# Thirty small loads that nobody reads, in two sets on SyncE's queue, in a decode attention kernel

## The chip, the cores and the metric

The kernel runs on one core of a Trainium2 chip. The metric is the device time of one execution in microseconds (us); the time shown is the median of three runs. The profile and the trace belong to one further execution, taken by the hardware profiler, and all times inside it count from its first instruction.

## The reference

One decode step of grouped-query attention, gated by a small dense network. With B = 2 sequences, one query position each, D = 512, 32 query heads, 8 key/value heads of 128 elements and 32768 cached positions, all in 32-bit floats:

```
xn  = layernorm(x)
q   = (xn @ wq), 32 heads of 128
s   = softmax(q . k_cache * 128**-0.5) . v_cache     # 4 query heads share one k/v head
s   = s @ wo
h   = relu(xn @ w1 + b1)**2
g   = silu(h @ w2 + b2)
out = x + s * g
```

The two caches hold 2 x 8 x 32768 x 128 floats each, and every element of them is read once.

## The kernel before, in words

**Tiling.** There are 16 pairs of sequence and key/value head, counted by s. The keys of a pair are loaded in two transfers, counted by m = 2s and 2s + 1, each of 128 partitions with 128 rows of 128 floats (8 MB); the values of a pair in two transfers of the same size, counted by j. Keys go into `kring`, a ring of three slots of 64 rows per partition, values into `vbuf`, which holds 128 rows per partition. A load of keys needs two slots of the ring, so it may only be issued when DVE has transposed what lay there (`transposed`, the counter KT[1]). A load of values may only be issued when TensorE has done with the values before (the counter PV).

**Engines.** DVE transposes keys out of `kring` into `kt` (line 309), in blocks of 128x4096. TensorE multiplies them with the query into `ps_s` (line 270), ScalarE copies the scores out (line 333), DVE and ScalarE make the softmax (lines 315, 318, 336), TensorE transposes the probabilities (line 299) and multiplies them with the values into `o_ps` (line 280). Lines 270 to 348 are helpers that the loops over s call.

**Order of the loads.** All large transfers are issued by SyncE (SP), in the order in which its program is written; the helper `load` (line 84) waits for the marks it is given and then issues one transfer, so a wait holds back all that SP has behind it. Every load counts its landing on a semaphore that rises by 16. SP's program is: `wq` into `vbuf` (line 138), keys 0 and one half of keys 1 (lines 139 and 140), then `w1` when the query is computed, the other half of keys 1, `w2`, keys 2 in two halves, values 0, keys 3, values 1, and then, pair by pair, keys m + 2 and values m. The last of these are keys 31 and values 29. Behind them stand the values of the last pair: values 30 into two slots of `kring` (named `va`, when the second last keys are transposed) and values 31 into `vbuf` (`vb`, when values 29 are used up), then the five pieces of `wo`: rows 0 to 15, 16 to 24, 25 to 28, 29 and 30, and 31. ScalarE issues four small loads at the start (x twice, b1, b2) and the store of the result at the end (line 587).

**The start.** ScalarE loads x into `kt`; the layer norm runs on DVE, TensorE transposes xn, DVE copies it to `xnT` (line 201), and TensorE computes the query (line 210) as soon as `xnT` and `wq` are there.

**The end.** `columns` and `columns4` (lines 525 and 533) multiply the attention's output with the pieces of `wo` as they land. Behind the last piece come two operations on DVE (lines 582 and 583) and the store. SP waits for the last piece, issues four idle instructions, waits for ScalarE's last instruction, clears the semaphores, and waits for the store (line 592).

The lines at which the change stands:

```
    wq_in = load(SP, wq_t, wq.rearrange("(p d) f -> p d f", p=P), dma("wq"))
    k0_in = load_k(0)
    load_k_half(1, 1)
...
    L = NH - 2
    va, vb = dma("va"), dma("vb")
    va_in = load(SP, kring[:, 0:2 * SLOT, :], v_rows(L), va, transposed(NQ - 2))
    vb_in = load(SP, vbuf, v_rows(L + 1), vb, PV.at(L))
...
    SP.wait(wo_in[31])
```

Of the kernel before, what the change touches and what calls it, by code (L numbers as in the profile page):

```python
# [5 lines left out]
F32 = mybir.dt.float32  # L6
# [46 lines left out]
def gqa_decode_kernel(nc, x, kc, vc, wq, wo, w1, b1, w2, b2, out):  # L53
# [20 lines left out]
    def bank(name, n=1):  # L74
# [3 lines left out]
    SP, ACT, DVE, POOL, TE = (Lane(nc, e, n) for e, n in (  # L78
        (nc.sync, "sp"), (nc.scalar, "act"), (nc.vector, "dve"), (nc.gpsimd, "pool"), (nc.tensor, "pe")))
    tensor, vector, scalar, gpsimd, sync = nc.tensor, nc.vector, nc.scalar, nc.gpsimd, nc.sync  # L80

    def load(lane, dst, src, sem, *marks):
        lane.wait(*marks)
        return sem.after(lane.eng.dma_start(dst, src))  # L84

    def dma(name):
        return Count(nc, name, 16)
# [9 lines left out]
    def k_rows(m):  # L97
        s, u = divmod(m, 2)
        return rows(kc, s).rearrange("(p u r) d -> p u r d", p=P, u=2)[:, u]

    def v_rows(j):
        s, u = divmod(j, 2)
        return rows(vc, s)[u * P * RUN:(u + 1) * P * RUN].rearrange("(p r) d -> p r d", p=P)
# [16 lines left out]
    def transposed(q):  # L120
        return KT[1].at(q + 1)

    def load_k_half(m, i, *marks):
        c = k_order(m)[i][1]
        return load(SP, k_slot(2 * m + i), k_rows(m)[:, c * SLOT:(c + 1) * SLOT], k_sems[m % 2], *marks)

    def load_k(m):
        a = m % 2
        return load(SP, kring[:, a * SLOT:(a + 2) * SLOT, :], k_rows(m), k_sems[a], transposed(max(2 * m - 2, -1)))
# [6 lines left out]
    wo_t = [kflat[:, a * SLOT * DH:a * SLOT * DH + 16 * D].rearrange("p (r e) -> p r e", r=16) for a in (2, 0)]  # L136

    wq_in = load(SP, wq_t, wq.rearrange("(p d) f -> p d f", p=P), dma("wq"))
    k0_in = load_k(0)
    load_k_half(1, 1)  # L140

# [133 lines left out]
    def te_values(vt, cs=(0, 1), first=True, last=True):  # L275
        for c in cs:
            for i in range(4):
                for g in range(NG):
                    lo = c * SLOT + g * NO + 4 * i
                    mm_ = tensor.matmul(o_ps[32 * g:32 * g + 16, :],  # L280
                                        pTh[:, 2 * g + c, 2 * i:2 * i + 2, :, :].rearrange("p o y h -> p (o y h)"),
                                        vt[:, lo:lo + 4, :].rearrange("p o d -> p (o d)"),
                                        start=(first and c == cs[0] and i == 0), stop=(last and c == cs[-1] and i == 3),
                                        skip_group_check=True)
        mm_.then_inc(PV.sem, 1)
# [52 lines left out]
    def act_probs(a0, *marks):  # L338
        ACT.wait(*marks)
        v = pT_ps.rearrange("p n (k x z a h) -> p x (n k) z a h", k=4, x=8, z=2, a=2, h=REP)  # L340
        for a in range(2):
            for y in range(2):
                i = scalar.copy(pTh[64 * a:64 * a + 64, :, :, y, :], v[64 * y:64 * y + 64, :, :, a0, a, :])  # L343
        PTH.after(i)
# [157 lines left out]
            set_q(s + 1)  # L502


    L = NH - 2
    va, vb = dma("va"), dma("vb")
    va_in = load(SP, kring[:, 0:2 * SLOT, :], v_rows(L), va, transposed(NQ - 2))
    vb_in = load(SP, vbuf, v_rows(L + 1), vb, PV.at(L))
    wo_r = wo.rearrange("(p r) e -> p r e", p=P)
    wo_in = {}  # L510

    def load_wo(r0, r1, *marks):
        wo_in[r0] = load(SP, wo_t[r0 // 16][:, r0 % 16:r0 % 16 + r1 - r0, :], wo_r[:, r0:r1, :], dma(f"wo{r0}"), *marks)

    load_wo(0, 16, transposed(NQ - 1))
    load_wo(16, 25, PV.at(L + 1))
    load_wo(25, 29)
# [20 lines left out]
    def spare(n):  # L538
        for _ in range(n):
            tensor.matmul(pj_ps[:, 0:P], ident, ident, start=True, stop=True)  # L540

    TE.wait(va_in, (PTH.sem, 16 * (L + 1)))
    te_values(kring[:, 0:2 * SLOT, :], first=True, last=False)
    act_probs(1, PV.at(L + 1))
    with nc.Fori(0, 9, 1, engines=[PE]):
        spare(4)
    TE.wait(vb_in, (PTH.sem, 16 * (L + 2)))
    te_values(vbuf, first=False, last=True)
# [25 lines left out]
    t = columns4(31, 32)  # L574

    spare(4)
    SP.wait(wo_in[31])
    idle = Count(nc, "idle")
    for _ in range(4):
        idle.after(sync.nop())  # L580
# [35 lines left out]
```

## Time and profile before

| what | value |
|---|---|
| median of 3 runs | 1303.49 us (1303.37 to 1303.68) |
| span of the profiled execution, first to last instruction | 1302.6 us |
| PE busy (matmuls) | 639.7 us, 49% |
| DVE busy | 619.0 us, 48% |
| ACT busy | 128.6 us, 10% |
| POOL busy | 11.9 us, 1% |
| bytes read from HBM | 561.01 MB, 431 GB/s over the span |

The profiled execution's span stands beside a median that is 0.9 us longer: what lies ahead of the first and behind the last instruction is in the runs' times and not in the span. Busy times are sums over the span; engines work beside each other, so the shares do not add up to one. "DMA" is the share of time in which the 16 DMA engines were moving packets. A queue named q1 is the one that SP's transfers go through, q10 that of ScalarE's, q8 and q14 bring in instructions.

### The profile page before, as it was taken

The page shows a single profiled execution, that of the slowest core. Times are in us where ns is not written, and L with a number is a line of the kernel's source. Part 1 is how long each engine was busy: PE and PEld are TensorE (multiplying, and loading weights), DVE is VectorE, ACT ScalarE, POOL GpSimd, SP SyncE. Part 2 cuts the span into 40 slices and gives each one's busy share as a digit, 9 for nine tenths or more (in the row PEclk, how much of TensorE's full clock was granted, in tenths as well). Part 3 has the DMA queues.
Part 4 walks back from the last instruction along what each step waited for, and adds up shares of the span by engine and source line. Part 5 has one row for each costly group of instructions (what it writes and reads, how often), then busy time and mean ns, then how long its engine had stood idle before and what let it go on. Part 6 is the DMA issues. An engine that isn't in the chain of part 4 may idle for free.

```text
span 1302.6 us, 10806 instructions
## 1 busy us (share of the span) xinstructions
PE 639.7 (49%) x4710; PEld 175.6 (13%) x4710; DVE 619.0 (48%) x305; ACT 128.6 (10%) x262; POOL 11.9 (1%) x41
## 2 busy tenths in 40 slices
PE   3555444555535455544536543444653444554368
PEld 1111110111101011110101111111110111111014
DVE  2565553436555344655435555343655534455410
ACT  0111011111001011000111101011100101101010
POOL 0000000000000000000000000000000000000000
PEclk9778677878767787777788777678877778877789
DMA  9999999999999999999999999999999999999998
GB/s 419 418 448 423 441 427 435 431 437 433 431 437 427 443 427 441 429 441 427 439 427 437 433 431 437 427 443 427 441 429 441 427 439 427 439 431 429 441 425 356
DMA packets 10703, 561.14 MB, mean 431 GB/s; under 512 B 1199, under 2 KB 1219, under 8 KB 1478
## 3 DMA queue, kind: packets, MB, share of 16 engines
q1 hardware_dynamic: 10656, 560.99, 99.6%
q8 instruction: 6, 0.10, 0.0%
q10 hardware_dynamic: 38, 0.02, 0.0%
q14 instruction: 3, 0.02, 0.0%
HBM read 561.01 MB, written 0.00 MB: 431 GB/s over the span
## 4 chain that ended last, share of the span: by engine, by line
DMA 77%; DVE 12%; issue 10%; PE 1%; SPq 0%; DVEq 0%
DMA kring<-in_A_k_cache 73%; DVE kt L309 12%; DMA kring<-in_A_v_cache 2%; DMA kring<-in_A_wo 2%; PE o_ps L280 1%; PE acc_ps L533 0%; PE pj_ps L540 0%; SPq L84 0%; DVEq L308 0%; PE acc_ps L411 0%
## 5 line engine op out<-in xcount | busy, mean ns | idle before, releaser
L309 DVE STREAM_TRANSPOSE kt<-kring 128x4096 f32<-128x4096 f32 x128 | 557.6, 4414 | 449.4 <-DMA kring<-in_A_k_cache 449.4
L270 PE MATMUL ps_s<-kt,qz 128*32 128x512 f32 x2048 | 333.5, 779 | 603.4 <-DVE kt L309 603.4
L280 PE MATMUL o_ps<-vbuf,pTh 128*16 128x512 f32 x1984 | 227.5, 612 | 1.8 <-DMA vbuf<-in_A_v_cache 1.8
L270 PEld LDWEIGHTS ps_s<-kt,qz 128*32 128x32 f32 x2048 | 67.8, 128 | 845.1 <-issue 669.9
L333 ACT ACTIVATE sc<-ps_s,halves 128x512 f32<-128x512 f32 x64 | 46.6, 729 | 866.5 <-PE ps_s L270 866.5
L280 PEld LDWEIGHTS o_ps<-vbuf,pTh 128*16 128x16 f32 x1984 | 57.8, 101 | 178.0 <-issue 158.6
L343 ACT COPY pTh<-pT_ps 64x256 f32<-64x256 f32 x128 | 46.9, 366 | 39.6 <-PE pT_ps L299 21.6
L315 DVE CUSTOM_DVE_ANT_0 sc<-sc 128x1024 f32<-128x1024 f32 x16 | 19.6, 1225 | 54.9 <-ACT sc L333 54.9
L318 DVE CUSTOM_DVE_ANT_0 junk<-mx_ps,other 128x128 f32<-128x128 f32 x16 | 4.7, 292 | 82.1 <-PE mx_ps L288 82.1
L336 ACT ACTIVATE sc<-sc,nm 128x1024 f32<-128x1024 f32 x16 | 18.4, 1149 | 108.9 <-DVE nm L318 108.9
L328 DVE TENSOR_REDUCE hr<-fin_ps 128x4 f32<-128x64 f32 x16 | 3.6, 225 | 48.5 <-PE fin_ps L292 48.5
L292 PE MATMUL fin_ps<-ident,o_sb 128*128 128x128 f32 x64 | 10.5, 286 | 17.4 <-DVE o_sb L485 17.2
L348 ACT COPY o_sb<-o_ps 128x512 f32<-128x512 f32 x15 | 8.8, 586 | 97.2 <-PE o_ps L280 97.2
L299 PE MATMUL pT_ps<-ident,sc 128*128 128x128 f32 x128 | 17.5, 282 | 0.0
L299 PEld LDWEIGHTS pT_ps<-ident,sc 128*128 128x128 f32 x128 | 15.3, 147 | 0.0
L280 PE MATMUL o_ps<-kring,pTh 128*16 128x512 f32 x64 | 9.3, 749 | 9.0 <-DMA kring<-in_A_v_cache 9.0
L493 POOL COPY oT<-ho 128x4 f32<-128x4 f32 x15 | 2.8, 188 | 1147.2 <-DVE ho L329 1147.2
L210 PE MATMUL pT_ps<-vbuf,xnT 128*32 128x512 f32 x64 | 8.5, 693 | 7.4 <-DMA vbuf<-in_A_wq 7.4
L227 DVE COPY kt<-pT_ps 128x512 f32<-128x512 f32 x8 | 5.0, 683 | 13.2 <-PE pT_ps L210 13.2
L540 PE MATMUL pj_ps<-ident 128*128 128x128 f32 x88 | 10.8, 278 | 0.0
L540 PEld LDWEIGHTS pj_ps<-ident 128*128 128x128 f32 x88 | 10.1, 192 | 1.9 <-issue 1.9
L485 DVE TENSOR_TENSOR o_sb<-o_sb,o_ps 128x512 f32<-128x512 f32 x15 | 10.2, 682 | 0.0
(90 smaller groups left out, 105.5 us busy)
## 6 DMA issues: line engine op xcount, KB each, us to landing
kring<-in_A_k_cache SPq DMA_DIRECT2D x4, 4096.0 KB, 23.8
vbuf<-in_B_w SPq DMA_DIRECT2D x2, 3584.0 KB, 28.5
kring<-in_A_wo SPq DMA_DIRECT2D x1, 4096.0 KB, 41.2
kring<-in_A_wo SPq DMA_DIRECT2D x1, 2304.0 KB, 25.5
kring<-in_A_wo SPq DMA_DIRECT2D x1, 1024.0 KB, 27.6
kring<-in_A_wo SPq DMA_DIRECT2D x1, 512.0 KB, 28.4
vbuf<-in_A_v_cache SPq DMA_DIRECT2D x31, 30.1
kring<-in_A_k_cache SPq DMA_DIRECT2D x30, 29.8
```

The costliest lines, as they stand in the source:

```text
L270: i = tensor.matmul(ps_s[32 * g:32 * g + 32, :], qz[:, 2 * y + e, :], kt[y][:, g * NO:(g + 1) * NO, 32 * e:32 * e + 32], start=(y == 0 and ...
L280: mm_ = tensor.matmul(o_ps[32 * g:32 * g + 16, :], pTh[:, 2 * g + c, 2 * i:2 * i + 2, :, :].rearrange("p o y h -> p (o y h)"), vt[:, lo:lo ...
L292: t = tensor.transpose(fin_ps[:, i * P:(i + 1) * P], o_sb[:, i * DH:(i + 1) * DH], ident)
L299: t = tensor.transpose(pT_ps[:, k // 4, (k % 4) * P:(k % 4 + 1) * P], p[:, k * P:(k + 1) * P], ident)
L309: KT[y].after(vector.transpose(kt[y], k_slot(q)[:, :, 64 * y:64 * y + 64]))
L315: return DVE(lambda: vector.tensor_tensor_reduce(scf[0], scf[0], scf[1], 1.0, -3.4e38, ALU.add, ALU.max, rm), mark, on=on)
L333: ACT(lambda: scalar.mul(sc[c][:, :, :, u], ps_s.rearrange("p (o w) -> p o w", w=32), halves[:, c:c + 1]), *marks, on=EV)
L336: return ACT(lambda: scalar.activation(scf[0], scf[0], AF.Exp, bias=nm, scale=SCALE, accum_out=l), mark, on=on)
L343: i = scalar.copy(pTh[64 * a:64 * a + 64, :, :, y, :], v[64 * y:64 * y + 64, :, :, a0, a, :])
L348: scalar.copy(o_sb, o_ps).then_inc(OE.sem, 32)
L485: DVE(lambda: vector.tensor_add(o_sb, o_sb, o_ps), on=OSR)
L540: tensor.matmul(pj_ps[:, 0:P], ident, ident, start=True, stop=True)
```

## The change

A tile `steps` of 15 partitions is added, and a function that issues 15 loads from SP. The k-th load, k = 1 to 15, brings k rows of 16 floats (64 B) of `w2` into column k - 1 of `steps`. Nothing reads `steps`. The first set stands behind the load of `wq` and ahead of keys 0; the second behind values 29 and ahead of values 30, and waits for the first set's landing. SP's last wait asks for the second set's landing too.

```diff
     wq_in = load(SP, wq_t, wq.rearrange("(p d) f -> p d f", p=P), dma("wq"))
+    steps = nc.alloc_sbuf_tensor("steps", (15, 15, 16), F32).ap()
+
+    def stairs(sem, *marks):
+        for k in range(1, 16):
+            have = load(SP, steps[0:k, k - 1, :], w2[0:k, 16 * k:16 * k + 16], sem, *marks)
+        return have
+
+    first_stairs = stairs(dma("stairs0"))
     k0_in = load_k(0)
     load_k_half(1, 1)
...
+    last_stairs = stairs(dma("stairs1"), first_stairs)
+
     L = NH - 2
     va, vb = dma("va"), dma("vb")
...
-    SP.wait(wo_in[31])
+    SP.wait(wo_in[31], last_stairs)
```

## Rows read from the trace of the kernel before

**Rows 1.** The page: span, DMA share, memory, and queues (packets, MB, share).
```profile
span 1302.6 us, 10806 instructions
...
DMA  9999999999999999999999999999999999999998
...
q1 hardware_dynamic: 10656, 560.99, 99.6%
q8 instruction: 6, 0.10, 0.0%
q10 hardware_dynamic: 38, 0.02, 0.0%
...
HBM read 561.01 MB, written 0.00 MB: 431 GB/s over the span
```

**Rows 2.** Windows: stretch, length, five engines' busy time, PE clock, DMA share, GB/s.
```profile
140.00:500.00 360.00, 175.56 (x1260) 44.86 (x1264) 183.04 (x85) 35.16 (x69) 3.09 (x10) 0.77 1.00 433
500.00:900.00 400.00, 199.88 (x1446) 50.15 (x1438) 192.50 (x86) 38.79 (x77) 3.08 (x10) 0.77 1.00 433
900.00:1200.00 300.00, 139.18 (x1000) 35.75 (x1000) 150.67 (x68) 29.33 (x59) 2.47 (x8) 0.77 1.00 433
1200.00:1260.00 60.00, 27.47 (x222) 7.49 (x222) 20.69 (x14) 6.87 (x14) 0.19 (x1) 0.81 1.00 435
```

**Rows 3.** Windows of the end, same columns as rows 2.
```profile
1297.50:1298.00 0.50, 0.30 (x12) 0.30 (x16) 0.47 (x1) 0.00 (x0) 0.00 (x0) 1.00 0.46 184
...
1298.70:1298.90 0.20, 0.20 (x12) 0.03 (x4) 0.00 (x0) 0.00 (x0) 0.00 (x0) 1.00 0.06 20
1298.90:1299.10 0.20, 0.20 (x12) 0.16 (x12) 0.00 (x0) 0.00 (x0) 0.00 (x0) 1.00 0.06 20
1299.10:1299.40 0.30, 0.30 (x16) 0.22 (x8) 0.00 (x0) 0.00 (x0) 0.00 (x0) 1.00 0.00 0
```

**Rows 4.** Timeline of all engines at the end: start us, us, engine, line.
```profile
1299.73 0.27 PE L533 MATMUL acc_ps<-kring,oR 128*32 128x128 f32 x1
...
1300.79 0.63 ACTq L587 DMA_DIRECT2D out<-fin  x1
```

**Rows 5.** Timeline of SP and ACT issues at the start, columns as in rows 4.
```profile
0.74 0.38 SPq L84 DMA_DIRECT2D vbuf<-in_A_wq  x1
1.17 0.90 SPq L84 DMA_DIRECT2D kring<-in_A_k_cache  x2
...
1.43 1.22 ACTq L84 DMA_DIRECT2D kt<-in_A_x  x1
...
3.03 0.25 ACTq L84 DMA_DIRECT2D b2t<-in_B_b  x1
```

**Rows 6.** Timeline of SP's issues at the end, columns as in rows 4.
```profile
1209.36 0.33 SPq L84 DMA_DIRECT2D vbuf<-in_A_v_cache  x1
1230.44 0.33 SPq L84 DMA_DIRECT2D kring<-in_A_v_cache  x1
1248.06 0.33 SPq L84 DMA_DIRECT2D vbuf<-in_A_v_cache  x1
...
1269.69 1.75 SPq L84 DMA_DIRECT2D kring<-in_A_wo  x4
```

**Rows 7.** Timeline: who starts on the loads' landings; in brackets idle time and releaser.
```profile
15.55 0.29 DVE L201 COPY xnT<-mx_ps 128x128 f32<-128x128 f32 x1 [1.22 <-PE mx_ps L200]
...
22.90 8.52 PE L210 MATMUL pT_ps<-vbuf,xnT 128*32 128x512 f32 x64 [7.38 <-DMA vbuf<-in_A_wq]
...
1240.94 0.13 PEld L280 LDWEIGHTS o_ps<-vbuf,pTh 128*16 128x16 f32 x8 [0.80 <-DMA vbuf<-in_A_v_cache]
...
1279.64 7.06 PE L280 MATMUL o_ps<-vbuf,pTh 128*16 128x512 f32 x64 [1.79 <-DMA vbuf<-in_A_v_cache]
```

**Rows 8.** DMA view of 1301.8 to 1302.3 us (the store): packets, then queue q10.
```profile
DMA packets 12, 0.00 MB, mean 8 GB/s; under 512 B 4, under 2 KB 12, under 8 KB 12
...
q10 hardware_dynamic: 12, 0.00, 3.4%
```

**Rows 9.** DMA view of 9.7 to 10.0 us: queue q10 (four packets, all under 512 B).
```profile
q10 hardware_dynamic: 4, 0.00, 0.8%
```

**Rows 10.** DMA view of 0 to 30 us: busy tenths, slices of 0.75 us.
```profile
DMA  0090009609904900900940990990290094098099
```

**Rows 11.** DMA issues of the last pieces of `wo`: KB, us from issue to landing.
```profile
kring<-in_A_wo SPq DMA_DIRECT2D x1, 512.0 KB, 28.4
kring<-in_A_wo SPq DMA_DIRECT2D x1, 256.0 KB, 28.5
```

## The prediction

> **What bounds the kernel now.** I read the page first [rows 1]. The DMA line is at nine tenths or more in 39 of 40 slices, and SP's queue alone fills 99.6% of 16 engines' span. 561.01 MB come in at a mean of 431 GB/s. No compute engine passes 49%. So this kernel lasts as long as its transfers do, if the rate is the most that the engines give. The windows say that it is [rows 2]: three long stretches with different loads in flight all give 433 GB/s at a DMA share of 1.00, and the best stretch gives 435. A shortage behind compute would show as a share below 1.00 in one of them, and none is there.
>
> Then I read the end [rows 3, 4]. The DMA share falls to 0.46 by 1298.0 us and is 0.06, one engine of sixteen, from 1298.7 to 1299.1 us; then it is nought. The engines do not end together: about half have finished more than 1 us before the last. The last multiplication starts at 1299.73 us, after the last landing, and the store is issued at 1300.79 us. What delays the engine that ends last therefore delays the end one for one, and what delays an engine that ends early, by less than its lead, delays nothing.
>
> **The change, part by part.** It removes nothing. It adds 30 issues on SP, 30 small loads in the rings, and two waits.
>
> *The issues of the first set.* SP issues `wq` at 0.74 us in 0.38 us, and the next two loads in 0.90 us [rows 5], so 0.33 us [rows 6] to 0.45 us each. Fifteen more take 4.9 to 6.8 us; at ScalarE's dearest, 1.22 us [rows 5], 18.3 us. Keys 0 are then issued at 6 to 8 us, at worst at 19.5 us. Data starts 0.8 to 1.5 us behind an issue: SP's first issue is at 0.74 us and the first busy slice is 1.5 to 2.25 us [rows 5, 10]. `wq` lands at 22.9 us [rows 7]. So keys 0 stand in the rings before `wq` has left them, by more than 10 us at the likely price and by about 2 us at the worst. Cost nothing; without that cover, 4.9 to 18.3 us. SP next waits for the query at about 30 us, long after.
>
> ScalarE's four loads at 1.43 to 3.9 us are issued beside SP's and could be held up. The longest of them took 1.22 us beside SP's, the shortest 0.25 us [rows 5]; a delay of x by 1 us or even 5 us moves `xnT` from 15.8 us towards 22.9 us, where TensorE waits for `wq` anyway [rows 7]: 7.0 us of slack. Cost nothing.
>
> *The issues of the second set.* SP issues values 29 at 1209.36 us and its next load, values 30, at 1230.44 us, when the keys before it have been transposed [rows 6]. Between them SP has 20.7 us in which it only waits. The set takes 4.9 to 6.8 us of these, at worst 18.3 us. Values 30 are not held back. The wait for the first set was met 1180 us before. The last wait asks for loads that lie in the rings ahead of values 30 and landed some 55 us earlier. Cost nothing.
>
> *The small loads in the rings.* This is the only part on the path. Rows of 64 B are not in the trace, so I bound them. The store's queue had 12 packets, 3.4% of 16 engines for 0.5 us, 0.27 us in all [rows 8]; four are landing marks of 4 B, eight are pieces of 512 B. Four marks alone are 0.8% of 16 engines for 0.3 us, so 9.6 ns each [rows 9]; the 512 B pieces are left with 29 ns each. A 64 B piece lies between, 9.6 to 29 ns, nearer the mark in size, so I take 9.6. With its landing mark a small load costs an engine 19 ns, at most 39 ns. An engine that takes part in all 15 loads of a set loses 0.29 us, at most 0.58 us; one that takes part in none loses nothing. ScalarE's queue has 38 packets for five transfers [rows 1], which fits one mark per engine used and one engine per row for the loads of one, two and four rows; so the load of k rows goes to k engines, and a set weighs on the engines unequally. Which engine ends last is in no row. I take half of the 15 loads for it, in both sets: 15 x 19 ns = 0.29 us. The ends are 0 (the last engine takes part in none, or all others stay within their lead) and 30 x 39 ns = 1.2 us.
>
> The Trainium skill says in DMA: Bandwidth & Descriptors, "Why a DMA increments its semaphore by 16 and not by 1", that a transfer of k rows runs on the lowest-numbered k engines; by that engine 0 takes part in all 15 loads of a set and engine 15 in none. No row here numbers the engines, and the sum would still lie between the same two ends.
>
> *Instruction fetches.* Thirty more instructions can move SP's fetches. The instruction queue shows six packets with 0.10 MB [rows 1], 17 KB each; at 431/16 = 27 GB/s one is 0.6 us of one engine. If the last engine gets one more or one fewer, that is plus or minus 0.6 us. I take nought and keep both ends. The tile `steps` moves other tiles to other addresses; no row shows a time that depends on an address: nothing.
>
> **The sum.** 1302.6 us of span and 0.3 us give 1302.9 us. The median of the runs is 0.9 us above the profiled execution's span [rows 1], so the forecast is 1303.8 us: no change that can be measured (about 0.2%, 2.6 us, can be told from none).
>
> **The rivals.**
>
> *Slower: the queue takes only so many loads.* In the trace SP never has more than six loads under way: at 1271.4 us values 31, which land at 1279.64 us, and five pieces of `wo`, the last four issued in 1.75 us without a stall [rows 6, 7]. The change asks for 18 at the start (`wq`, 15 small ones, keys 0, half of keys 1). If SP has to stop at some number, it stops until `wq` has landed at 22.9 us, and the rings run dry while it issues the rest. At a limit of 6 that is ten more small loads and keys 0 at 0.33 us each and 0.8 to 1.5 us until data: 4.4 to 5.1 us. Behind values 29, which land at 1240.9 us [rows 7], the same comes again. Together 9 to 10 us: about 1313 us. At a limit of 16 it is 0.33 us and 0.8 to 1.5 us twice, 3 us: 1306.5 us. It decides from a limit of 16 downwards. For it: nothing in the trace reaches beyond six. Against it: six large loads bring more pieces per engine than many small ones, and SP was not held. Chance 0.07.
>
> *Much slower: a small load holds its ring for a whole round trip.* The store takes at most 1.8 us from its issue at 1300.79 us to the end of the span [rows 1, 4]. An engine in all 30 loads would lose 54 us: about 1357 us. Against it: the last two pieces of `wo` were issued some 0.44 us apart and took 28.4 and 28.5 us [rows 11], so they landed 0.5 us apart, no round trip between them. Chance 0.02.
>
> The Trainium skill (DMA: Bandwidth & Descriptors, "Anatomy of one DMA — SWDGE (gpsimd) path") gives a transfer a fixed cost of about 2.0 us, and its "Rules for kernel authors" call transfers under 64 KB mostly overhead; charged thirty times in a row that would be an estimated 60 us, some 1364 us. The trace disagrees where loads queue behind each other, with the same 0.5 us.
>
> *Faster: the small loads push the engines apart, and these get in each other's way less.* The most to be had is the best rate, 435 for 433 GB/s from 140 to 1200 us [rows 2]: 1060 x 2/435 = 4.9 us, 1298.6 us. For it: the engines differ in what the set gives them. Against it: the rate is the same in three stretches, the engines are already more than 1 us apart at the end [rows 3], and a set moves them by 0.3 us; 435 is one short stretch, in which a few packets at the edges make the difference. Chance 0.04.
>
> **How the numbers follow.** The forecast has 0.87, and with the rivals' 0.07, 0.02 and 0.04 that is all. Faster takes the third rival, slower the first two. The range is the forecast's own: below, 1303.5 less 0.6 us for a fetch and 0.1 us for the runs' spread, 1302.8; above, 1303.5 and 1.2 and 0.6 us and 0.2 us of spread, 1305.5. The rivals lie outside it, with little else.
>
> **What would show it right or wrong.** Right: 30 more issues on SP, 15 within 5 to 7 us behind `wq` and 15 between values 29 and values 30; the query still starts near 22.9 us and values 30 are issued near 1230.4 us; the stretches keep 433 GB/s; the last multiplication starts within 1.5 us of 1299.7 us. If the queue has a limit, one small issue of SP lasts until `wq` lands, and the DMA line has a gap behind 22.9 and behind 1240.9 us. If a small load holds its ring, the landings of keys 0 and values 30 come tens of us late. A faster kernel would show more than 433 GB/s in the long stretches; a stretch at a lower rate without a gap, or a later end with neither, would prove the working wrong.

## The result, and the profile after

The changed kernel takes 1306.64 us (median of 10 runs, 1306.45 to 1306.81) where the kernel before took 1303.66 us in the same comparison (10 runs, 1303.37 to 1303.74). It is slower by 2.98 us, a ratio of 1.0023 with a 95% interval of 1.0015 to 1.0031. The forecast was 1303.8 us, with a range from 1302.8 to 1305.5 us.

First the page of the changed kernel, which answers to [rows 1], and the windows of its long stretches, which answer to [rows 2].

```profile
span 1305.3 us, 10836 instructions
...
q1 hardware_dynamic: 11136, 561.01, 99.6%
q8 instruction: 6, 0.10, 0.0%
```

```profile
140.00:500.00 360.00, 172.89 (x1254) 44.54 (x1254) 182.93 (x84) 35.15 (x69) 3.08 (x10) 0.78 1.00 434
500.00:900.00 400.00, 190.50 (x1439) 49.59 (x1443) 193.89 (x87) 38.61 (x76) 3.08 (x10) 0.80 1.00 433
900.00:1200.00 300.00, 139.38 (x1009) 35.72 (x1004) 149.32 (x68) 29.55 (x59) 2.46 (x8) 0.76 1.00 433
```

SP's queue has 480 packets more: two sets of 120 rows, with as many landing marks, as many as there would be if a load of k rows goes to k engines. Between the sets nothing has changed: 433 to 434 GB/s. The 2.98 us must lie at the sets. Next SP's issues, which answer to [rows 5, 6].

```profile
1.17 5.50 SPq L84 DMA_DIRECT2D steps<-in_B_w  x15
6.72 0.87 SPq L84 DMA_DIRECT2D kring<-in_A_k_cache  x2
...
1210.70 0.33 SPq L84 DMA_DIRECT2D vbuf<-in_A_v_cache  x1
1211.08 5.24 SPq L84 DMA_DIRECT2D steps<-in_B_w  x15
1231.79 0.35 SPq L84 DMA_DIRECT2D kring<-in_A_v_cache  x1
```

The issues cost what was forecast, 5.2 and 5.5 us, and both are covered. Then the timeline of who starts on the landings, which answers to [rows 7], and the end, which answers to [rows 4].

```profile
22.92 1.94 PE L218 MATMUL pT_ps<-vbuf,xnT 128*32 128x512 f32 x8 [7.51 <-DMA vbuf<-in_A_wq]
...
44.67 17.43 DVE L317 STREAM_TRANSPOSE kt<-kring 128x4096 f32<-128x4096 f32 x4 [10.13 <-DMA kring<-in_A_k_cache]
...
1242.49 0.13 PEld L288 LDWEIGHTS o_ps<-vbuf,pTh 128*16 128x16 f32 x8 [1.00 <-DMA vbuf<-in_A_v_cache]
...
1263.43 9.95 PE L288 MATMUL o_ps<-kring,pTh 128*16 128x512 f32 x64 [10.61 <-DMA kring<-in_A_v_cache]
...
1282.79 7.06 PE L288 MATMUL o_ps<-vbuf,pTh 128*16 128x512 f32 x64 [1.17 <-DMA vbuf<-in_A_v_cache]
...
1303.54 0.63 ACTq L597 DMA_DIRECT2D out<-fin  x1
```

Two rows of the kernel before that were not shown yet stand against them, the first keys and values 30:

```profile
43.30 17.43 DVE L309 STREAM_TRANSPOSE kt<-kring 128x4096 f32<-128x4096 f32 x4 [9.26 <-DMA kring<-in_A_k_cache]
...
1260.29 9.32 PE L280 MATMUL o_ps<-kring,pTh 128*16 128x512 f32 x64 [9.03 <-DMA kring<-in_A_v_cache]
```

The query starts within 0.02 us of before. Keys 0, the first large load behind a set, are used 1.37 us later; values 29 are still 1.55 us late; values 30, the first large load behind the second set, are 3.14 us late; values 31 3.15 us and the store 2.75 us. So each set delays the one large load behind it by about 1.5 us, and nothing of that is won back between the sets; of the 3.15 us, 0.40 are won back between values 31 and the store.

What happens there shows in the DMA view of three short windows (packets, MB, and the packets' whole time as a share of 16 engines over the window). The view counts a packet, with its whole length, where it starts; so a share can pass 100%. From 1240.74 to 1240.92 us only one engine's small packets start, and from 1240.92 to 1240.93 us one packet, the large one behind them. From 1241.62 to 1241.63 us one landing mark and one large packet start, behind another engine's set.

```profile
DMA packets 27, 0.00 MB, mean 5 GB/s; under 512 B 27, under 2 KB 27, under 8 KB 27
...
q1 hardware_dynamic: 27, 0.00, 9.3%
```

```profile
q1 hardware_dynamic: 1, 0.07, 2410.0%
```

```profile
q1 hardware_dynamic: 2, 0.07, 2658.8%
```

The 27 small packets are recorded with 9.3% x 16 x 0.18 us = 0.27 us, 9.9 ns each, and one starts 6.7 ns behind another: 13 ns for a load with its mark, less than the 19 ns of the prediction. But the large packet of 64 KB behind them is recorded with 24.10 x 16 x 0.01 us = 3.86 us, and the other engine's with 26.59 x 16 x 0.01 us = 4.25 us. In the kernel before, 10 such packets that start from 12.1 to 12.4 us make up 503.8%:

```profile
q1 hardware_dynamic: 10, 0.66, 503.8%
```

That is 2.42 us each. The loss, 1.44 us on one engine and 1.83 us on the other, is in the record of the first large packet behind a set, not in the records of the small ones.

### The profile page after: what moved, and what is told of

The parts are those of the page before. It is cut to its first block, busy times and chain, and to the rows that moved or that the text cites. A ratio compares the mean times of both kernels' runs of the same rounds, so it can differ in the third digit from the quotient of the medians.

```text
span 1305.3 us, 10836 instructions
## 1 busy us (share of the span) xinstructions
PE 629.5 (48%) x4710; PEld 175.1 (13%) x4710; DVE 619.0 (47%) x305; ACT 128.6 (10%) x262; POOL 11.9 (1%) x41
## 4 chain that ended last, share of the span: by engine, by line
DMA 77%; DVE 12%; issue 10%; PE 1%; SPq 0%; DVEq 0%
DMA kring<-in_A_k_cache 72%; DVE kt L317 12%; DMA kring<-in_A_v_cache 2%; DMA kring<-in_A_wo 2%; PE o_ps L288 1%; SPq L84 0%; PE acc_ps L543 0%; PE pj_ps L550 0%; DVEq L316 0%; PE acc_ps L419 0%
## 5 line engine op out<-in xcount | busy, mean ns | idle before, releaser
L278 PE MATMUL ps_s<-kt,qz 128*32 128x512 f32 x2048 | 324.4, 760 | 615.7 <-DVE kt L317 615.7
L288 PE MATMUL o_ps<-vbuf,pTh 128*16 128x512 f32 x1984 | 224.6, 605 | 1.3 <-DMA vbuf<-in_A_v_cache 1.2
```

The lines of the kernel that those rows point to most:

```text
L278: i = tensor.matmul(ps_s[32 * g:32 * g + 32, :], qz[:, 2 * y + e, :], kt[y][:, g * NO:(g + 1) * NO, 32 * e:32 * e + 32], start=(y == 0 and ...
L288: mm_ = tensor.matmul(o_ps[32 * g:32 * g + 16, :], pTh[:, 2 * g + c, 2 * i:2 * i + 2, :, :].rearrange("p o y h -> p (o y h)"), vt[:, lo:lo ...
```

## The experiments

Three theories stood at first: A, B and C, as the first expectation states them; B was split in two (B1, B2) ahead of the fifth run. All differences below are between medians of one comparison, of the experiment's runs and those of the kernel before on the same chip. The runs of one kernel lie within 0.9 us of each other, mostly within 0.5 us; the intervals of the ratios are wider, plus or minus 0.0009 to 0.0017, which is 1.2 to 2.2 us. For five small effects below (the first set alone, the second alone, the single load with 16 pieces per engine, four loads, 24 spread loads) the interval reaches 1.0000; what they cost rests on where the single runs lie. The diffs show the lines that make the difference, those with `range(4)`, with `range(8)`, with 128 rows and with 512 B against the kernel with 15 loads of 16 rows, the one behind the loads of values against the kernel before, all others against the changed kernel; the size of `steps` and waits that go with it are left out.

**One set at a time.** First set only, and second set only:

```diff
-    last_stairs = stairs(dma("stairs1"), first_stairs)
-    SP.wait(wo_in[31], last_stairs)
+    SP.wait(wo_in[31], first_stairs)
```

> Only the first set is kept. Theory A (an engine reads ahead a limited number of packets; a burst of small ones fills that number with hardly any bytes, so the first large packet behind the burst is read late): half the loss, 1.2 to 1.7 us over the kernel before; keys 0 land about 1.4 us late, as in the changed kernel, and nothing is added behind values 29. Rival B (each separate load costs its engine a fixed change-over at its landing mark): the same. Rival C (the loss comes from the engines being pushed apart, and grows with the distance): less than a third, under 1.0 us, since the second set pushes furthest.

```diff
-    first_stairs = stairs(dma("stairs0"))
-    last_stairs = stairs(dma("stairs1"), first_stairs)
+    last_stairs = stairs(dma("stairs1"))
```

> Only the second set is kept. A and B: 1.3 to 1.8 us over the kernel before; values 29 land where they landed before (TensorE starts near 1240.9 us), values 30 about 1.5 us late. C: under 1.0 us. If the two sets alone do not add up to the 3.0 us of both, the sets act on each other.

The first alone costs 1.34 us (ratio 1.0010, 1.0000 to 1.0019), the second 1.18 us (1.0009, 0.9999 to 1.0018). Every run of both lies above all 27 runs of the kernel before (at most 1303.96 us; the lowest here is 1304.55 us). Keys 0 are used 1.25 us later than before in the first (1.4 us expected), values 30 1.25 us later in the second (1.5 us expected). Both costs are above the 1.0 us that C allowed, and 0.46 us short of the 2.98 us together. That points at the sets acting on each other, but 0.46 us is less than the intervals are wide. The single packet records of the second-only kernel give the excess over 2418 ns of the packets that start from 1238.5 to 1243.3 us. The 15 loads of a set weigh on the engines by 15, 14, 13 and so on down to none, and the longest excesses in ns fall in the same way:

```
1810 1613 1387 1335 1244 1231 1043 923 410 280 84 27 15 14 13 8 ...
```

Taken in order, 15 loads go with 1.8 us, 8 loads with 0.9 us, and four or fewer with next to nothing. The order is a reading, as the records do not name the engine; it can be checked once, in the changed kernel: the 27 small packets above are 13 pieces with 14 marks, and the 1.44 us behind them are the third longest excess of that kernel, where the order puts 13 loads.

**Every engine alike, and one mark in place of 15.**

```diff
-        for k in range(1, 16):
-            have = load(SP, steps[0:k, k - 1, :], w2[0:k, 16 * k:16 * k + 16], sem, *marks)
+        for k in range(15):
+            have = load(SP, steps[:, k, :], w2[0:16, 16 * k:16 * k + 16], sem, *marks)
```

> Both sets, but each of the 15 loads has 16 rows, one for every engine, so that no engine is pushed ahead of another by them. A and B: every engine loses what the most loaded one lost, 1.5 to 2.2 us a set, 3.0 to 4.4 us in all. C: under 0.6 us, only the small packets' own time (15 x 13 ns x 2 = 0.4 us).

```diff
-    steps = nc.alloc_sbuf_tensor("steps", (15, 15, 16), F32).ap()
+    steps = sb("steps", 2, 32)
...
+        return load(SP, steps[:, :, 0:16], w2[0:P, 0:64].rearrange("p (a b) -> p a b", a=2)[:, :, 0:16], sem, *marks)
```

> Each set is one single load of 128 partitions with two pieces of 64 B each: 16 small pieces on each of the 16 engines, and one landing mark in place of 15. A: 17 packets in place of 30 in the burst, so about 17/30 of the loss of the kernel with 15 loads of 16 rows: 1.7 to 2.6 us in all. B: one load in place of 15: under 0.4 us. C: under 0.5 us.

Fifteen loads of 16 rows cost 4.60 us (1.0034, 1.0021 to 1.0046), 2.3 us a set. C falls: pushing no engine ahead of another costs more, not less. A single load with 16 pieces per engine costs 0.51 us (1.0004, 0.9994 to 1.0014), 0.26 us a set. Theory A, in the form in which packets fill the read-ahead, asked for 1.7 us or more and falls for this size. The windows from 1236 to 1246 us, ten us around the second set, show the same, first with 15 loads of 16 rows, then in the kernel before (last column GB/s):

```profile
1236.00:1246.00 10.00, 6.21 (x56) 1.63 (x60) 6.89 (x4) 0.75 (x1) 0.00 (x0) 1.00 1.04 362
```

```profile
1236.00:1246.00 10.00, 7.69 (x72) 1.83 (x68) 4.30 (x3) 0.75 (x1) 0.00 (x0) 1.00 1.03 446
```

At 433 GB/s the missing 84 GB/s over 10 us are 1.9 us. That is a rough figure: a packet is counted where it starts, and one more large packet on each of the 16 engines makes 105 GB/s over ten us. The packets' own records are sharper: the 16 first large packets behind the second set, one for each engine, are 1.41 to 2.27 us longer than 2.418 us, 1.78 us in the mean. The DMA share is above 1.00 in both windows: the stretched packets count as busy for their whole length, so the share does not show the loss.

**How many, and how close together.** Fifteen replaced by 4 and by 8 loads of 16 rows, and 24 such loads one by one behind the loads of values:

```diff
-        for k in range(15):
+        for k in range(4):
```

> Both sets with 4 loads of 16 rows in place of 15. In the runs so far the first large packet behind n small loads on one engine came late by about 1.8 us at 15, 1.0 us at 8 or 9 and almost nothing up to 4. Theory B2 (what a small load costs is its own transfer with its landing mark, some 0.13 us of an engine; the first few are hidden by what the engine has read ahead, and beyond that they add up): 0.0 to 0.4 us over the kernel before. B1 (every load costs the same 0.13 us wherever it stands): 2 x 4 x 0.15 = 1.2 us.

```diff
-        for k in range(15):
+        for k in range(8):
```

> Both sets with 8 loads of 16 rows. B2: about 0.9 to 1.3 us a set on the late engines, 1.8 to 2.6 us in all if all engines lose alike. B1: 2 x 8 x 0.15 = 2.4 us. Theory A (packets fill the read-ahead): 17 packets, like the single load with 16 pieces, so the 0.5 us that this one lost.

```diff
             if m + 2 < NH:
                 load_k(m + 2)
                 load_v(m)
+                if m < 26:
+                    load(SP, steps[:, m - 2, :], w2[0:16, 16 * (m - 2):16 * (m - 2) + 16], steps_sem)
```

> No set; 24 small loads of 16 rows stand one by one, each behind a load of values in the loop. B2: each is hidden alone, only the packets' own time is left, 24 x 13 ns = 0.3 us: 0.0 to 0.6 us over the kernel before. B1: 24 x 0.15 = 3.6 us.

Four loads cost 0.22 us (1.0002, 0.9992 to 1.0011), eight 1.84 us (1.0014, 1.0004 to 1.0024), 24 spread ones 0.51 us (1.0004, 0.9994 to 1.0014). B1 falls: at a fixed price the four would have cost 1.2 us and the spread ones 3.6 us. From 4 to 8 loads a load adds (1.84 - 0.22)/8 = 0.20 us, from 8 to 15 (4.60 - 1.84)/14 = 0.20 us; a load among the first four 0.03 us, a load standing alone 0.02 us. The first four and the lone loads cannot be told from nothing but their own packets' time. B2's threshold and its straight line behind it are as expected; its price of 0.13 us was too low. In the records behind the second set the mean excess of the 16 packets is 0.04 us for four loads, 0.63 for eight and 1.78 for 15: 0.15 to 0.16 us a load. The time goes by the engine that ends last, the records' mean does not, so the two prices need not be the same.

A falls here once more, at equal counts: eight loads put 16 small packets on each engine and cost 1.84 us, the single load put 17 there and cost 0.51 us.

**Pieces against loads.** Fifteen loads with eight pieces per engine each:

```diff
-            have = load(SP, steps[:, k, :], w2[0:16, 16 * k:16 * k + 16], sem, *marks)
+            have = load(SP, steps[:, k, :], w2[0:P, 16 * k:16 * k + 16], sem, *marks)
```

> Both sets of 15 loads, each of 128 rows of 64 B: 8 pieces and one mark per engine and load. If the cost per load is a fixed step behind its pieces (they add to each other), the pieces' time of 7 x 6.5 ns a load comes on top of the 4.6 us of the kernel with 16 rows: 4.6 + 2 x 15 x 0.046 = 6.0 us. If the fixed time of a load runs beside its pieces, 4.6 us again. Theory A, by packets (135 for 30): above 9 us.

This cost 6.51 us (1.0051, 1.0034 to 1.0068), near the 6.0 us of the first case, but for another reason. The timeline of SP's issues in this kernel:

```profile
0.74 0.38 SPq L84 DMA_DIRECT2D vbuf<-in_A_wq  x1
1.17 21.57 SPq L84 DMA_DIRECT2D steps<-in_B_w  x15
22.79 0.91 SPq L84 DMA_DIRECT2D kring<-in_A_k_cache  x2
...
1212.40 31.02 SPq L84 DMA_DIRECT2D steps<-in_B_w  x15
1243.47 0.43 SPq L84 DMA_DIRECT2D kring<-in_A_v_cache  x1
```

Narrower windows of the same timeline give the first eight small loads, and the ninth:

```profile
1.17 4.15 SPq L84 DMA_DIRECT2D steps<-in_B_w  x8
```

```profile
5.37 14.51 SPq L84 DMA_DIRECT2D steps<-in_B_w  x1
```

SP is held inside the set: the first eight small loads go out by 5.3 us, and the ninth takes until 19.9 us. Behind `wq`, with 9 packets per engine, the eight have put 72 more into each ring. This is the prediction's slower rival, a queue that takes only so much, at a size that the change does not reach: its fullest ring holds `wq`, 30 small packets, keys 0 and half of keys 1, 57 packets, and SP issued all of them without a stall. It is no limit on the number of loads: SP was held here at the tenth, and the changed kernel took 18. Values 30 were issued at 1243.47 us in place of about 1231 us, so the 6.51 us contain a queue that ran dry (from 23.28 to 23.55 us no packet starts), and the run says nothing on the question it was made for. The next kernel has the same pieces in one load:

```diff
+        return load(SP, steps, w2[0:P, 0:480].rearrange("p (a b) -> p a b", a=15)[:, :, 0:16], sem, *marks)
```

> Both sets as one single load of 128 partitions with 15 pieces of 64 B each: on every engine the same 120 pieces of 64 B as in the kernel with 15 loads of 128 rows, but one landing mark, one transfer, in place of 15. If the loss goes by loads (theory B2), only the pieces' own time is left, 2 x 120 x 6.5 to 7 ns = 1.6 to 1.7 us over the kernel before, and little behind it: 1.5 to 2.3 us. If it goes by packets (theory A, in any form in which small packets fill what an engine reads ahead), the 121 packets in place of 135 lose nearly what the 15 loads lost: 5.5 to 6.5 us.

The 120 pieces in one load cost 3.30 us (1.0025, 1.0015 to 1.0035), 1.65 us a set. SP is held in this kernel too, at the issue of keys 0, until 22.81 us:

```profile
1.65 21.16 SPq L84 DMA_DIRECT2D kring<-in_A_k_cache  x1
```

So 1.65 us is an upper bound for what the pieces cost. Both expectations missed. A price by packets is at most 1.65 us/121 = 13.6 ns each, about twice the 6.5 to 7 ns at which they are recorded one behind another. But 121 packets in one load lose less than 30 packets in 15 loads (2.3 us). Taking 30 x 13.6 ns = 0.4 us off, at least 1.9 of those 2.3 us go by the load.

**Are they slow because they are small?** Pieces of 512 B in place of 64 B, with the same count:

```diff
-            have = load(SP, steps[:, k, :], w2[0:16, 16 * k:16 * k + 16], sem, *marks)
+            g = 16 * (k % 8)
+            have = load(SP, steps[g:g + 16, k // 8, :], w2[0:16, 16 * k:16 * k + 128], sem, *marks)
```

> Both sets of 15 loads of 16 rows, with pieces of 512 B in place of 64 B: the same loads, packets and marks, eight times the bytes. If the loss came from pieces being under 512 B, it goes: only their own time is left, 2 x 15 x (23 + 6.5) ns = 0.9 us over the kernel before, at most 1.5 us. If it goes by loads and a load's fixed time comes behind its piece, the longer pieces add 2 x 15 x 17 ns = 0.5 us to the 4.6 us of the 64 B pieces: 5.1 us; if the fixed time runs beside the piece: 4.6 us.

These cost 4.92 us (1.0036, 1.0022 to 1.0051), as much as the 64 B pieces to within 0.3 us. The size of the pieces, 64 or 512 B, is not the cause. Nor are the partitions that are written: these loads go in turn to eight groups of 16 partitions, the 64 B pieces all went to the same 16. Whether the longer piece adds to a load's fixed time or runs beside it is left open between 4.6 and 5.1 us.

## Why the prediction was wrong

**The step that failed** is "The small loads in the rings". It took 19 ns for a load and its mark, at most 39 ns, out of the lengths at which packets are recorded [rows 8, 9]. Those lengths were right, and even generous: 9.9 ns measured for the 9.6 ns taken, and a load with its mark passes in 13 ns. But a recorded length is not what a packet costs the ones behind it. Beyond the fourth in a burst, a load of one piece per engine costs its engine 0.20 us, ten times the term, and the profile books it on the next large packet. At 19 ns an engine that takes part in all 30 loads would lose 0.6 us, at 39 ns 1.2 us; the kernel with equal loads shows 4.60 us. So the term stood in the sum with 0.29 us, and 2.98 us were measured. The prediction named a stretch at a lower rate without a gap as what would prove its working wrong; the ten us around the second set, with 362 GB/s in the kernel with equal loads and 446 in the kernel before, are such a stretch.

**The share of the last engine.** The prediction gave the last engine half of the loads. In the changed kernel the two sets cost 1.5 us each where equal loads cost 2.3 us: the engine that ends last is not the one with all 15 loads, or that one had a lead to use up. The sums would agree with leads: alone the sets cost 1.34 and 1.18 us, together 2.98 us, 0.46 us more than the two, as when the first set uses up a lead that the second no longer finds. That is argued from the sums, within their intervals, and not shown; the engines could not be told apart by name.

**What held.** SP's issues (4.9 to 6.8 us forecast, 5.2 and 5.5 us measured), both covers, the untouched start of the query, the untouched rate in the long stretches, the instruction fetches (six packets on q8 in both kernels), and the rule that a delay of the last engine is a delay of the end: the last large packet ends at 1301.84 in place of 1299.09 us, and the store is issued 2.75 us later, as much.

**The rivals.** The limit of the queue exists, but was not met. Its 1306.5 us for a limit of 16 loads lie next to the measured 1306.64 us by chance: SP issued all 18 loads by 7.6 us and was never held. The faster rival asked for more than 433 GB/s in the long stretches, and there were 433 to 434. The round trip that a small load holds its ring for had the right form, a fixed step per load, at the wrong size: 1.8 us were set for it, 0.20 us were measured. What spoke against it, the last two pieces of `wo` landing 0.5 us apart [rows 11], cannot speak against 0.20 us: one load alone costs 0.02 us, and a set of four next to nothing.

The Trainium skill (DMA: Bandwidth & Descriptors, "Anatomy of one DMA — SWDGE (gpsimd) path") lays the fixed cost of about 2.0 us that it measured for transfers issued by GpSimd mostly to the confirmation of the last write. The loads here are issued by SP. Charged thirty times in a row the 2.0 us would have been an estimated 60 us; the runs show 0.20 us per load in a burst and 0.02 us alone, so the figure is not what a load adds in the ring of this kernel. The Trainium skill (the same title, "Specifications") wants at least 512 B for line rate; the pieces of 512 B lost as much as those of 64 B here (4.92 and 4.60 us), so that rule is not what was met.

**Left open.** Whether the 0.20 us belong to the landing mark or to the change from one transfer to the next was not tried: no run has loads without marks. The small loads of a burst also read next to one another in the same rows of `w2`, and no run reads elsewhere; but the loads that stood alone, at 0.02 us each, and the one load of 120 pieces an engine read there too. Why about four are free is not shown either; an engine that has read ahead and can wait that long without losing anything would explain it, and no run tests that.

## What to carry to other kernels

Where the DMA engines are the bound, count the separate loads that stand directly behind each other in a ring, not their bytes: in this kernel the fifth and later ones of a burst cost 0.2 us each, while a single one between large loads cost 0.02 us. Put small loads apart, or make one load of many pieces out of them (16 pieces in one load: 0.26 us; 15 loads of one piece: 2.3 us). And price a new kind of transfer by what the next large packet loses, not by the length of its own record.

## What the runs showed of the hardware that was not expected

- A large packet's record can stretch from 2.42 to 4.25 us behind a set of small loads in the changed kernel. With 15 loads of 16 rows the DMA share over the ten us around the second set is 1.04, against 1.03 before; only the rate in GB/s falls, from 446 to 362.
- SP can be held while it issues, which is read here as a full queue. Behind 9 packets per engine it issued eight loads of 9 packets per engine at once and was held at the ninth for 14.5 us.
